# In a fused attention, feed-forward and expert kernel, two-source SBUF work is moved from GpSimd to VectorE for the feed-forward part

## The chip, the core and the metric

The kernel runs on one core of a Trainium2 chip. The metric is the device time of one execution in microseconds (us). Before the change the median of three runs is 783.74 us (783.47 to 784.02).

## What is computed

The reference runs three stages one after the other: a linear attention with exponential features, a layer that mixes along the sequence and then applies a feed-forward network, and an expert layer. Cut to what matters here:

```python
def phi(x):
    proj = np.einsum('bhsd,df->bhsf', x, w_phi)          # b 4, h 8, s 576, d 64, f 128
    proj = proj - np.max(np.abs(proj), axis=-1, keepdims=True)
    return np.concatenate([np.exp(proj), np.exp(-proj)], axis=-1)
# attention: x = (phi(q) @ (phi(k)^T v)) / (phi(q) . sum phi(k) + 1e-6)      -> (4, 576, 512)

h = x.transpose(0, 2, 1) @ U @ V                          # rank 32
u = x + h.transpose(0, 2, 1)
x = u + np.maximum(u @ w_ch1, 0.0) @ w_ch2                # 512 -> 2048 -> 512

# experts: each token takes one of 8 (argmax of x @ w_gate, or the one of the token before)
out[b, s] = p[e] * (np.maximum(x[b, s] @ w1[e], 0.0) @ w2[e])
```

The weights `U`, `V`, `w_ch1` and `w_ch2` come as float64; the kernel narrows them to float32 itself. `w1` and `w2` are float32.

## The kernel before

**Stages.** The program is one long list of instructions, built by a Python planner. The attention stage runs to about 203 us. The feed-forward network follows as twelve items: the 2048 hidden features are cut into four units (`ffn_units`, each of 512 features), and each unit is applied to three pieces of 768 tokens (`NP = 3`); a piece has two token blocks of 384 (`TW`). Item 0 is spread through the attention stage. Eight expert items follow (two units for each batch entry, blocks of 288). In the trace, items 1 to 2 take 206 to 272.6 us, items 3 to 5 take 272.6 to 372.4, items 6 to 8 take 372.4 to 466.4, and items 9 to 11 run on to 562 us, with the routing of the tokens to experts between their steps.

**One matrix product.** TensorE multiplies float32 in three passes: each operand is split in a high part (float32r) and the rest, and `three` (lines 965 to 976) issues high by high, high by rest and rest by high. So each weight piece `f` needs a copy on ScalarE (`w_end`, line 344) and a subtraction (lines 345 and 346, which ends in line 71 or line 338); each token block needs the same (`x_end`, lines 512 and 515). Items 4 to 11 use seven products in place of eight for the first matrix (`seven_steps`), which needs sums and differences of weight blocks (`sums`, lines 374 to 376) and of token blocks (`x_sums`, `sub`, lines 548 to 551).

**Work on the result.** The sums of `seven_steps` (line 943, `u`, `psf`), the ReLU with its split (line 959 on ScalarE, line 945 on VectorE) and the addition to `y` (line 943, `y`) read PSUM. TensorE needs them soon.

**Narrowing a weight piece.** `fetch` (lines 311 to 331) takes a raw float64 piece of 128x512 that SyncE's queue has loaded, and `narrow` (lines 80 to 104) turns it to float32 in six VectorE instructions, lines 89, 92, 95, 97, 99 and 102, and one addition on GpSimd in two halves of 256 (`in_halves`, line 71). Line 89 clears the sign bit of the high words. Units 1, 2 and 3 are narrowed beside the items: eight pieces each.

**Who does what.** `either` (lines 196 to 217) gives a two-source operation on SBUF to GpSimd or to VectorE, whichever the planner's clock has done sooner, with one microsecond (`BIAS`) against VectorE. On GpSimd it is cut in halves; on VectorE it is one instruction, line 338 for 512 columns. GpSimd's queue also issues the loads of saved token blocks from DRAM (`x_load`, line 578); SyncE's queue issues the stores of blocks (line 518), the raw weights (line 305) and `row` loads (line 544).

**What sets the order.** The planner keeps a modelled clock for each engine (`free`), a time for each buffer (`touched`) and one for the work that `either` places (`port`). Every engine runs its instructions in the order in which they were emitted. `gate` (lines 182 to 194) emits a step when its modelled end is not later than TensorE's modelled time plus `SLACK`, which has a value for each engine and each step of an item; for VectorE it is 0 to 2.5 us. When TensorE needs a weight or a block that isn't there, `until` (line 250) forces it out. `fetch` waits until two of the eight `row` buffers are free (line 315), and `x_load` and `x_end` take from nine token-block buffers (`xfree`). The expert items don't use `fetch`.

Of the kernel before, what the change touches and what calls it, by code (L numbers as in the profile page):

```python
# [39 lines left out]
def model(ctx, tc, kq, vx, wphi, ident, up, vp, wff, wg, wmoe1, wmoe2, rconst, outT):  # L40
# [23 lines left out]
    rawfree = [raw_p.tile([128, 1024], U32, name=f"raw{n}") for n in range(2)]  # L64

    pauses = [False]
    landed, wire = [0.0], [0.0]

    def paused(eng, **kw):
# [5 lines left out]
    def in_halves(eng, dst, a, b, n, op):  # L75

        for sl in (slice(0, n // 2), slice(n // 2, n)):
            paused(eng, out=dst[:, sl], in0=a[:, sl], in1=b[:, sl], op=op)

    def narrow(dst, raw, p, n, a=None, own=None):  # L80


        hw, lw = raw[:, 1::2], raw[:, 0::2]
        fine = own is not None
        own = own or [rows.pop(0) for _ in range(1 + (a is None))]
        a = own[1][:p, :n] if a is None else a
        b = own[0][:p, :n]
        au, bu = a.bitcast(U32), b.bitcast(U32)
        nc.vector.tensor_scalar(out=au, in0=hw, scalar1=0x7FFFFFFF, scalar2=None, op0=ALU.bitwise_and)  # L89
        if fine:  # L90
            yield
        nc.vector.tensor_scalar(out=b, in0=a, scalar1=F64_LO, scalar2=F64_MAX, op0=ALU.max, op1=ALU.min)
        if fine:
            yield
        nc.vector.tensor_scalar(out=au, in0=bu, scalar1=3, scalar2=0x3FFFFFFF, op0=ALU.logical_shift_left, op1=ALU.bitwise_and)
        yield
        nc.vector.scalar_tensor_tensor(out=au, in0=hw, scalar=0xC0000000, in1=au, op0=ALU.bitwise_and, op1=ALU.bitwise_or)
        yield
        nc.vector.tensor_scalar(out=bu, in0=au, scalar1=0xFF800000, scalar2=None, op0=ALU.bitwise_and)
        if fine:  # L100
            yield
        nc.vector.scalar_tensor_tensor(out=b, in0=lw, scalar=2.0 ** -52, in1=b, op0=ALU.mult, op1=ALU.mult)  # L102
        in_halves(nc.gpsimd, dst, a, b, n, ALU.add)
        rows.extend(own)

    def load_small(src, p, n):
# [36 lines left out]
    def x_tile(pool, n):  # L143
# [19 lines left out]
             "ACT": (0.3, 1.8, 1.8, 1.8, 0.5, 0.0, 0.5, 2.0, 2.0, 2.0, 2.0, 2.0, 2.0, 2.0, 2.0),  # L163
             "POOL": (2.0,) * 15}
    BIAS = 1.0
    at_step = [7]

    def cost(eng, n):
        return {"DVE": (0.075 + n / 960) * 1.15, "ACT": 0.17 + n / 1330, "POOL": 0.05 + n / 340}[eng]

    def of(eng):
        return "POOL" if eng is nc.gpsimd else "DVE"
# [9 lines left out]
    def gate(eng, dur, *keys):  # L182

        if not late:
            yield "step"
        while late and not force[0]:
            at = max([free[eng]] + [touched.get(id(k), 0.0) for k in keys])
            if at + (0.0 if eng == "POOL" else dur) <= free["PE"] + SLACK[eng][at_step[0]]:
                break
            yield "wait"  # L190
        emitted[0] += 1
        force[0] = False
        if late:
            book(eng, dur, *keys)

    def either(eng, n, *keys):

        if not late:
            yield "step"
            emitted[0] += 1  # L200
            return eng
        while True:
            best = None
            for e, name, bias in ((nc.gpsimd, "POOL", 0.0), (nc.vector, "DVE", BIAS)):
                dur = cost(name, n)
                at = max([free[name], port[0]] + [touched.get(id(k), 0.0) for k in keys])
                ok = at + (0.0 if name == "POOL" else dur) <= free["PE"] + SLACK[name][at_step[0]]
                if (ok or force[0]) and (best is None or at + dur + bias < best[0]):
                    best = (at + dur + bias, e, name, dur)
            if best is not None:  # L210
                break
            yield "wait"
        emitted[0] += 1
        force[0] = False
        free[best[2]] = max(free[best[2]], port[0])
        port[0] = book(best[2], best[3], *keys)
        return best[1]
# [89 lines left out]
            raws.append((u, name, t))  # L307

    pieces = {}

    def fetch(u, names):

        for name in names:
            raw_dma()
            while not raws or raws[0][:2] != (u, name) or len(rows) < 2:
                yield "blocked"
                raw_dma()
            t, f = raws.pop(0)[2], rows.pop(0)
            if wff.dtype == F32:
                yield from gate("POOL", cost("POOL", 512), t, f)  # L320
                nc.gpsimd.tensor_copy(out=f[:, :512], in_=t.bitcast(F32)[:, :512])
            else:
                g = yield from take(rows)
                parts = narrow(f[:, :512], t, 128, 512, f[:, :512], [g])
                for n_ in range(6):
                    yield from gate("DVE", 0.72 if n_ in (3, 5) else 0.46, t, f)
                    next(parts, None)
                book("POOL", cost("POOL", 512), f)
            rawfree.append(t)
            raw_dma()  # L330
            pieces[u, name] = f

# [173 lines left out]
    def x_end(key, s, r, keep, own=None, then=None):  # L506

        x = xo.setdefault(key, {})[s] = yield from take(xfree)
        n_ = CH if key[0] == "m" else TW
        keys = (x,) if own is None else (x, own)  # L510
        yield from gate("ACT", cost("ACT", 2 * n_), *keys)
        nc.scalar.copy(out=x[:, 0, :, :n_], in_=r)  # L512
        for k in range(2):
            use = yield from either(nc.gpsimd, n_, *keys)
            paused(use, out=x[:, 1, k, :n_], in0=r[:, k], in1=f32(x[:, 0, k, :n_]), op=ALU.subtract)
        if keep:
            def send():
                nc.sync.dma_start(out=f32(xd[key[1]][XD.index(s)]), in_=f32(x))
                if late:
                    transfer(768)  # L520
            later(x, send)
        xdone.add((key, s))
        if then is not None:
            then()
# [10 lines left out]
    def x_sums(key, due):  # L535
# [2 lines left out]

        def load(s):
            r = got[s] = yield from take(rows)  # L540
            while touched.get(id(r), 0.0) > free["PE"] + 0.5 and not force[0]:
                yield "wait"
            k, t = spot(key, s)
            nc.sync.dma_start(out=as_x(r), in_=ud[:, k, t])
            emitted[0] += 1
            touched[id(r)] = max(transfer(384), touched.get(id(r), 0.0) + 3.5)
# [21 lines left out]
        rows.append(got["B22"])  # L568
        end("T4", got["B21"])

    def x_load(key, names=XS):

        for s in names:
            x = xo.setdefault(key, {})[s] = yield from take(xfree)
            while touched.get(id(x), 0.0) > free["PE"] + 0.3 and not force[0]:
                yield "wait"
            yield from gate("POOL", 0.6, x)
# [333 lines left out]

    def x_first(key, due):

        yield from x_load(key, ("B11",))
        yield from x_sums(key, due)
        yield from x_load(key, ("B21", "B22"))

    def x_next(i):

# [315 lines left out]
    def side(i, step, steps):  # L1235

        u, b = items[i]
        if not late:
            return
        pauses[0] = i < NP or i > nf - NP  # L1240
        at_step[0] = 8 if steps == 16 else step
        k = units.index(u)
        if u.kind == "moe":
# [257 lines left out]
```

## Time and profile before

| | |
|---|---|
| median of three runs | 783.74 us |
| profiled execution | 781.76 us |
| its span, first to last instruction | 779.7 us |
| mean granted TensorE clock | 0.999 |
| TensorE busy | 763.8 us, 98% of the span |
| VectorE busy | 482.7 us, 62% |
| GpSimd busy | 362.2 us, 46% |
| ScalarE busy | 300.7 us, 39% |

The profiled execution is 1.98 us under the median, and its span is 2.06 us shorter than its own time. A difference worked out in the trace is taken off the median as it is. In rows of groups the first number after the bar is the busy time of all instructions of the group, the second the mean of one. A line can be a helper's: line 71 is every GpSimd subtraction or addition on SBUF, line 943 every VectorE sum that reads PSUM.

### The profile page before, as it was taken

The numbers are of one execution on the slowest core, as the hardware profiler recorded it, in microseconds if no ns is written. First come the engines' busy times: TensorE is split into PE (matmuls) and PEld (weight loads), VectorE is DVE, ScalarE is ACT, GpSimd is POOL, SyncE is SP. The second block draws the span as 40 slices with busy tenths as digits, with TensorE's granted clock in tenths as the row PEclk, the third lists the DMA queues.
The fourth block names the chain that finished last, engine by engine and source line by source line (L and its number), as shares of the span: only waits on it lengthen the run. The fifth ranks groups of instructions, "written<-read, shape, count | busy, mean of one in ns | idle before, by whom it ended". The sixth has DMA issues, their size and how long they took to land.

```text
span 779.7 us, 19252 instructions
## 1 busy us (share of the span) xinstructions
PE 763.8 (98%) x7776; PEld 741.6 (95%) x7776; DVE 482.7 (62%) x921; ACT 300.7 (39%) x682; POOL 362.2 (46%) x463
## 2 busy tenths in 40 slices
PE   8999999999999999899999999999999999999997
PEld 6899988999999999898999999999999999999997
DVE  7899999742488779897796865255643632203212
ACT  6667777652322131212213122023365164333420
POOL 1212423112477567574278532003566777866612
PEclk9999999999999999999999999999999999999999
DMA  6434556222342727591634807442453433434201
GB/s 200 153 125 160 207 178 227 71 104 82 136 169 82 277 88 278 195 340 65 228 120 162 301 1 270 152 146 82 131 186 97 133 102 102 125 122 127 79 1 63
DMA packets 45115, 114.34 MB, mean 147 GB/s; under 512 B 5024, under 2 KB 21536, under 8 KB 45024
## 3 DMA queue, kind: packets, MB, share of 16 engines
q1 hardware_dynamic: 36416, 82.74, 30.9%
q0 software_dynamic: 5152, 26.89, 10.2%
q10 hardware_dynamic: 3456, 3.46, 1.3%
q8 instruction: 62, 1.02, 0.5%
q14 instruction: 29, 0.24, 0.1%
HBM read 81.47 MB, written 31.60 MB: 145 GB/s over the span
## 4 chain that ended last, share of the span: by engine, by line
PE 82%; DVE 9%; issue 4%; POOL 2%; ACT 2%; POOLq 0%; DMA 0%; DVEq 0%; ACTq 0%
PE psf L1087 11%; PE psf L1089 11%; PE psf L1088 11%; PE psf L972 11%; PE psf L971 11%; PE psf L973 10%; PE kv L709 4%; PE pj L676 3%; PE num L743 3%; PE tq L723 2%; POOL row L71 1%; PE tps L769 1%; PE utps L786 1%; DVE row L89 1%; DVE pg L680 1%
## 5 line engine op out<-in xcount | busy, mean ns | idle before, releaser
L1087 PE MATMUL psf<-hhi,w 128*128 128x384 f32 (+1 forms) x640 | 204.6, 320 | 1.6 <-DVE hlo L945 1.6
L1088 PE MATMUL psf<-hhi,w 128*128 128x384 f32 (+1 forms) x640 | 203.7, 318 | 0.0
L1089 PE MATMUL psf<-hlo,w 128*128 128x384 f32 (+1 forms) x640 | 203.6, 318 | 0.0
L971 PE MATMUL psf<-x,w 128*128 128x384 f32 (+1 forms) x608 | 194.2, 319 | 3.0 <-DVE u L943 3.0
L972 PE MATMUL psf<-x,w 128*128 128x384 f32 (+1 forms) x608 | 193.9, 319 | 0.0
L973 PE MATMUL psf<-x,w 128*128 128x384 f32 (+1 forms) x608 | 193.9, 319 | 0.0
L945 DVE SCALAR_TENSOR_TENSOR hlo<-psf,hhi 128x384 fp32r<-128x384 f32 (+1 forms) x160 | 78.9, 514 | 145.9 <-ACT hhi L959 145.6
L71 POOL TENSOR_TENSOR w<-row,w 128x256 fp32r<-128x256 f32 x122 | 97.3, 809 | 92.8 <-ACT w L344 39.1
L959 ACT ACTIVATE hhi<-psf 128x384 fp32r<-128x384 f32 (+1 forms) x160 | 70.3, 461 | 176.6 <-PE psf L973 85.3
L71 POOL TENSOR_TENSOR row<-row,row 128x256 f32<-128x256 f32 (+1 forms) x105 | 89.1, 869 | 99.4 <-DVE row L102 91.1
L1087 PEld LDWEIGHTS psf<-hhi,w 128*128 128x128 f32 x640 | 120.1, 188 | 3.4 <-DVE hlo L945 2.3
L943 DVE TENSOR_TENSOR y<-psf,y 128x384 f32<-128x384 f32 (+1 forms) x128 | 67.0, 528 | 86.0 <-PE psf L1089 82.0
L1088 PEld LDWEIGHTS psf<-hhi,w 128*128 128x128 f32 x640 | 120.1, 188 | 0.0
L1089 PEld LDWEIGHTS psf<-hlo,w 128*128 128x128 f32 x640 | 120.1, 188 | 0.0
L971 PEld LDWEIGHTS psf<-x,w 128*128 128x128 f32 x608 | 114.3, 188 | 4.9 <-DVE u L943 4.0
L972 PEld LDWEIGHTS psf<-x,w 128*128 128x128 f32 x608 | 114.2, 188 | 0.3 <-POOL x L71 0.3
L973 PEld LDWEIGHTS psf<-x,w 128*128 128x128 f32 x608 | 114.2, 188 | 0.0
L71 POOL TENSOR_TENSOR x<-y,x 128x288 fp32r<-128x288 f32 (+1 forms) x56 | 51.9, 930 | 85.2 <-ACT x L512 78.2
L71 POOL TENSOR_TENSOR w<-raw,w 128x256 fp32r<-128x256 f32 x72 | 54.5, 757 | 32.6 <-ACT w L344 16.1
L344 ACT CAST w<-row 128x512 fp32r<-128x512 f32 x61 | 36.3, 622 | 76.7 <-POOL row L71 31.5
L679 DVE TENSOR_REDUCE mx<-pj 128x6 f32<-128x768 f32 (+2 forms) x49 | 45.8, 935 | 5.8 <-PE pj L676 5.7
L680 DVE TENSOR_TENSOR pg<-pj,mx 128x768 f32<-128x768 f32 (+2 forms) x49 | 46.1, 941 | 2.5
(110 smaller groups left out, 950.3 us busy)
## 6 DMA issues: line engine op xcount, KB each, us to landing
x<-xd POOLq DMA_DIRECT2D x34, 768.0 KB, 6.4
xd<-x SPq DMA_DIRECT2D x22, 768.0 KB, 4.5
raw<-in_wff SPq DMA_DIRECT2D x32, 512.0 KB, 3.3
raw<-in_wmoe SPq DMA_DIRECT2D x37, 256.0 KB, 2.7
kq<-in_kq SPq DMA_DIRECT2D x14, 576.0 KB, 3.9
row<-in_wmoe SPq DMA_DIRECT2D x27, 256.0 KB, 2.9
vt<-in_vx SPq DMA_DIRECT2D x16, 325.0 KB, 3.3
ud<-y SPq DMA_DIRECT2D x4, 1152.0 KB, 6.8
```

The costliest lines, as they stand in the source:

```text
L71: eng.tensor_tensor(**kw)
L679: nc.vector.tensor_reduce(out=mx[:, :, sl], in_=ps[:, :, sl], axis=AX, op=ALU.max, apply_absolute_value=True)
L680: nc.vector.tensor_tensor(out=p[:, :, sl], in0=ps[:, :, sl], in1=mx[:, :, sl].unsqueeze(3).to_broadcast([128, 2, m, 128]), op=ALU.subtract)
L943: nc.vector.tensor_tensor(**kw)
L945: nc.vector.scalar_tensor_tensor(op1=op1, **kw)
L959: at = act(lambda: nc.scalar.activation(out=hhi, in_=src, func=ACTF.Relu), n_, ready)
L971: nc.tensor.matmul(ps, lhsT=w[:, 0, c], rhs=x[:, 0, k, :n_], start=(first and k == 0), stop=False, skip_group_check=True)
L972: nc.tensor.matmul(ps, lhsT=w[:, 0, c], rhs=x[:, 1, k, :n_], start=False, stop=False, skip_group_check=True)
L973: nc.tensor.matmul(ps, lhsT=w[:, 1, c], rhs=x[:, 0, k, :n_], start=False, stop=(stop and k == 1), skip_group_check=True)
L1087: nc.tensor.matmul(ps, lhsT=wh, rhs=hhi, start=(k == 0), stop=False)
L1088: nc.tensor.matmul(ps, lhsT=wl, rhs=hhi, start=False, stop=False)
L1089: nc.tensor.matmul(ps, lhsT=wh, rhs=hlo, start=False, stop=(k == 3))
```

## The change

Up to the last but one feed-forward item (`lean`, item index below 11) `either` may choose VectorE alone, so that every sum, difference and split of weights and token blocks that was issued to GpSimd goes to VectorE as one instruction. GpSimd keeps the loads of line 578. The last addition of `narrow` goes through `either` as well. Line 89, which cleared the sign on VectorE, becomes an `Abs` on ScalarE for the pieces that `fetch` narrows. In the planner, VectorE's cost loses a factor of 1.15, the narrowing steps are booked at 0.37 and 0.62 in place of 0.46 and 0.72, and a VectorE step under `gate` is booked on `port` too. Two counters (`wanted`) keep rows and token-block buffers free for the start of a new set of token blocks (`x_first`). The attention stage, item 11 and the expert items keep their rules, apart from the new costs.

```diff
--- before.py
+++ after.py
@@ -64,6 +64,7 @@
     rawfree = [raw_p.tile([128, 1024], U32, name=f"raw{n}") for n in range(2)]
 
     pauses = [False]
+    pick = [nc.gpsimd]
     landed, wire = [0.0], [0.0]
 
     def paused(eng, **kw):
@@ -86,9 +87,11 @@
         a = own[1][:p, :n] if a is None else a
         b = own[0][:p, :n]
         au, bu = a.bitcast(U32), b.bitcast(U32)
-        nc.vector.tensor_scalar(out=au, in0=hw, scalar1=0x7FFFFFFF, scalar2=None, op0=ALU.bitwise_and)
         if fine:
+            nc.scalar.activation(out=a, in_=hw.bitcast(F32), func=ACTF.Abs)
             yield
+        else:
+            nc.vector.tensor_scalar(out=au, in0=hw, scalar1=0x7FFFFFFF, scalar2=None, op0=ALU.bitwise_and)
         nc.vector.tensor_scalar(out=b, in0=a, scalar1=F64_LO, scalar2=F64_MAX, op0=ALU.max, op1=ALU.min)
         if fine:
             yield
@@ -100,7 +103,12 @@
         if fine:
             yield
         nc.vector.scalar_tensor_tensor(out=b, in0=lw, scalar=2.0 ** -52, in1=b, op0=ALU.mult, op1=ALU.mult)
-        in_halves(nc.gpsimd, dst, a, b, n, ALU.add)
+        if fine:
+            yield
+        if pick[0] is nc.vector:
+            nc.vector.tensor_tensor(out=dst, in0=a, in1=b, op=ALU.add)
+        else:
+            in_halves(nc.gpsimd, dst, a, b, n, ALU.add)
         rows.extend(own)
 
     def load_small(src, p, n):
@@ -163,10 +171,11 @@
              "ACT": (0.3, 1.8, 1.8, 1.8, 0.5, 0.0, 0.5, 2.0, 2.0, 2.0, 2.0, 2.0, 2.0, 2.0, 2.0),
              "POOL": (2.0,) * 15}
     BIAS = 1.0
+    lean = [False]
     at_step = [7]
 
     def cost(eng, n):
-        return {"DVE": (0.075 + n / 960) * 1.15, "ACT": 0.17 + n / 1330, "POOL": 0.05 + n / 340}[eng]
+        return {"DVE": 0.085 + n / 960, "ACT": 0.17 + n / 1330, "POOL": 0.05 + n / 340}[eng]
 
     def of(eng):
         return "POOL" if eng is nc.gpsimd else "DVE"
@@ -184,14 +193,18 @@
         if not late:
             yield "step"
         while late and not force[0]:
-            at = max([free[eng]] + [touched.get(id(k), 0.0) for k in keys])
+            at = max([free[eng], port[0] if eng == "DVE" else 0.0] + [touched.get(id(k), 0.0) for k in keys])
             if at + (0.0 if eng == "POOL" else dur) <= free["PE"] + SLACK[eng][at_step[0]]:
                 break
             yield "wait"
         emitted[0] += 1
         force[0] = False
         if late:
-            book(eng, dur, *keys)
+            if eng == "DVE":
+                free[eng] = max(free[eng], port[0])
+            at = book(eng, dur, *keys)
+            if eng == "DVE":
+                port[0] = at
 
     def either(eng, n, *keys):
 
@@ -204,8 +217,8 @@
             for e, name, bias in ((nc.gpsimd, "POOL", 0.0), (nc.vector, "DVE", BIAS)):
                 dur = cost(name, n)
                 at = max([free[name], port[0]] + [touched.get(id(k), 0.0) for k in keys])
-                ok = at + (0.0 if name == "POOL" else dur) <= free["PE"] + SLACK[name][at_step[0]]
-                if (ok or force[0]) and (best is None or at + dur + bias < best[0]):
+                ok = (name == "DVE" or not lean[0]) and at + (0.0 if name == "POOL" else dur) <= free["PE"] + SLACK[name][at_step[0]]
+                if (ok or force[0] and (name == "DVE" or not lean[0])) and (best is None or at + dur + bias < best[0]):
                     best = (at + dur + bias, e, name, dur)
             if best is not None:
                 break
@@ -307,12 +320,13 @@
             raws.append((u, name, t))
 
     pieces = {}
+    wanted = [0, 0]
 
     def fetch(u, names):
 
         for name in names:
             raw_dma()
-            while not raws or raws[0][:2] != (u, name) or len(rows) < 2:
+            while not raws or raws[0][:2] != (u, name) or len(rows) < 2 + wanted[0]:
                 yield "blocked"
                 raw_dma()
             t, f = raws.pop(0)[2], rows.pop(0)
@@ -323,10 +337,18 @@
                 g = yield from take(rows)
                 parts = narrow(f[:, :512], t, 128, 512, f[:, :512], [g])
                 for n_ in range(6):
-                    yield from gate("DVE", 0.72 if n_ in (3, 5) else 0.46, t, f)
+                    if n_:
+                        yield from gate("DVE", 0.62 if n_ in (3, 5) else 0.37, t, f)
+                    else:
+                        yield from gate("ACT", cost("ACT", 512), t, f)
                     next(parts, None)
-                book("POOL", cost("POOL", 512), f)
-            rawfree.append(t)
+                rawfree.append(t)
+                raw_dma()
+                pick[0] = yield from either(nc.gpsimd, 512, f)
+                next(parts, None)
+                pick[0] = nc.gpsimd
+            if wff.dtype == F32:
+                rawfree.append(t)
             raw_dma()
             pieces[u, name] = f
 
@@ -506,6 +528,7 @@
     def x_end(key, s, r, keep, own=None, then=None):
 
         x = xo.setdefault(key, {})[s] = yield from take(xfree)
+        wanted[1] -= then is not None
         n_ = CH if key[0] == "m" else TW
         keys = (x,) if own is None else (x, own)
         yield from gate("ACT", cost("ACT", 2 * n_), *keys)
@@ -538,6 +561,7 @@
 
         def load(s):
             r = got[s] = yield from take(rows)
+            wanted[0] -= 1
             while touched.get(id(r), 0.0) > free["PE"] + 0.5 and not force[0]:
                 yield "wait"
             k, t = spot(key, s)
@@ -568,10 +592,13 @@
         rows.append(got["B22"])
         end("T4", got["B21"])
 
-    def x_load(key, names=XS):
+    def x_load(key, names=XS, first=False):
 
         for s in names:
+            while not first and len(xfree) <= wanted[1]:
+                yield "blocked"
             x = xo.setdefault(key, {})[s] = yield from take(xfree)
+            wanted[1] -= first
             while touched.get(id(x), 0.0) > free["PE"] + 0.3 and not force[0]:
                 yield "wait"
             yield from gate("POOL", 0.6, x)
@@ -911,9 +938,11 @@
 
     def x_first(key, due):
 
-        yield from x_load(key, ("B11",))
+        wanted[0] += 4
+        wanted[1] += 7
+        yield from x_load(key, ("B11",), True)
         yield from x_sums(key, due)
-        yield from x_load(key, ("B21", "B22"))
+        yield from x_load(key, ("B21", "B22"), True)
 
     def x_next(i):
 
@@ -1238,6 +1267,7 @@
         if not late:
             return
         pauses[0] = i < NP or i > nf - NP
+        lean[0] = i < nf - 1
         at_step[0] = 8 if steps == 16 else step
         k = units.index(u)
         if u.kind == "moe":
```

## Rows read from the trace of the kernel before

**Rows 1.** The page's engine table: busy us, share, instructions.

```profile
PE 763.8 (98%) x7776; PEld 741.6 (95%) x7776; DVE 482.7 (62%) x921; ACT 300.7 (39%) x682; POOL 362.2 (46%) x463
```

**Rows 2.** TensorE's waits, 195 to 525 us: us, times, longest.

```profile
PE psf L971 <- DVE u L943: 3.0, 3, 2.0
PE psf L1087 <- DVE hlo L945: 1.6, 1, 1.6
```

**Rows 3.** TensorE's timeline, first and last of four waits: start, us, instruction.

```profile
314.35 0.44 PE L971 MATMUL psf<-x,w 128*128 128x384 f32 x1 [2.00 <-DVE u L943]
...
411.83 0.45 PE L971 MATMUL psf<-x,w 128*128 128x384 f32 x1 [0.67 <-DVE u L943]
```

**Rows 4.** Engines' busy us (instructions) in items 1-8, then 3-5.

```profile
206.00:466.40 260.40, 255.71 (x1468) 254.02 (x1467) 207.94 (x342) 65.76 (x125) 162.43 (x192) 1.00 0.51 183
272.60:372.40 99.80, 95.78 (x549) 94.71 (x548) 82.72 (x129) 25.36 (x48) 61.72 (x71) 1.00 0.53 189
```

**Rows 5.** Timeline of VectorE, then GpSimd, around 335 us.

```profile
334.50 4.49 DVE L89 TENSOR_SCALAR row<-raw 128x512 uint32<-128x512 uint32 x1
...
334.75 3.94 POOL L71 TENSOR_TENSOR x<-row,x 128x384 fp32r<-128x384 f32 x4
```

**Rows 6.** VectorE's timeline where GpSimd is idle.

```profile
432.27 0.69 DVE L97 SCALAR_TENSOR_TENSOR row<-raw,row 128x512 uint32<-128x512 uint32 x1
432.97 0.56 DVE L943 TENSOR_TENSOR y<-psf,y 128x384 f32<-128x384 f32 x1
433.44 0.42 DVE L99 TENSOR_SCALAR row<-row 128x512 uint32<-128x512 uint32 x1
433.89 0.69 DVE L102 SCALAR_TENSOR_TENSOR row<-raw,row 128x512 f32<-128x512 uint32 x1
```

**Rows 7.** VectorE's narrowing by form, 195 to 525 us: busy us, mean ns.

```profile
L97 DVE SCALAR_TENSOR_TENSOR row<-raw,row 128x512 uint32<-128x512 uint32 x24 | 21.6, 900 | 0.4
L102 DVE SCALAR_TENSOR_TENSOR row<-raw,row 128x512 f32<-128x512 uint32 x24 | 19.8, 826 | 0.3
L95 DVE TENSOR_SCALAR row<-row 128x512 uint32<-128x512 uint32 x24 | 18.8, 784 | 0.6
L89 DVE TENSOR_SCALAR row<-raw 128x512 uint32<-128x512 uint32 x24 | 16.9, 703 | 0.0
L92 DVE TENSOR_SCALAR row<-row 128x512 f32<-128x512 f32 x24 | 16.3, 677 | 3.9 <-POOL row L71 2.8 <-DVE row L89 0.2
L99 DVE TENSOR_SCALAR row<-row 128x512 uint32<-128x512 uint32 x24 | 13.6, 567 | 0.3
```

**Rows 8.** GpSimd's work by form, 195 to 525 us.

```profile
L71 POOL TENSOR_TENSOR row<-row,row 128x256 f32<-128x256 f32 x68 | 55.8, 837 | 47.5 <-DVE row L102 44.0 <-POOL row L71 0.6 <-DVE w L338 0.6
L71 POOL TENSOR_TENSOR w<-row,w 128x256 fp32r<-128x256 f32 x56 | 47.2, 862 | 36.6 <-ACT w L344 34.4 <-POOL w L71 1.3 <-issue 0.6
L71 POOL TENSOR_TENSOR row<-row,row 128x384 f32<-128x384 f32 x21 | 22.0, 1077 | 4.8 <-DMA row<-ud 4.8
L71 POOL TENSOR_TENSOR x<-row,x 128x384 fp32r<-128x384 f32 x16 | 16.6, 1057 | 2.4 <-ACT x L512 2.4
L71 POOL TENSOR_TENSOR x<-y,x 128x384 fp32r<-128x384 f32 x12 | 12.4, 1041 | 17.4 <-ACT x L512 15.9 <-issue 1.1 <-POOL x L71 0.2
```

**Rows 9.** VectorE's splits of weights, then of tokens: ns min/median/max.

```profile
L338 DVE TENSOR_TENSOR w<-row,w x8: 681/1166/2626, 264.3 to 712.9; 128x512 fp32r<-128x512 f32 x8
...
L71 DVE TENSOR_TENSOR x<-row,x x8: 544/873/1359, 297.8 to 430.0; 128x384 fp32r<-128x384 f32 x8
```

**Rows 10.** Timeline: unit 2's last split, its second matrix's first matmul.

```profile
373.71 1.64 POOL L71 TENSOR_TENSOR w<-row,w 128x256 fp32r<-128x256 f32 x2 [6.40 <-ACT w L344]
...
388.00 0.45 PE L1087 MATMUL psf<-hhi,w 128*128 128x384 f32 x1
```

**Rows 11.** ScalarE's groups by form, whole run: copy, table load.

```profile
L344 ACT CAST w<-row 128x512 fp32r<-128x512 f32 x61 | 36.3, 622 | 76.7 <-POOL row L71 31.5 <-PE psf L1089 25.9 <-issue 14.7
...
L687 ACT ACT_TABLE_LOAD x1 | 1.3, 1283 | 1.2 <-PEq L1490 1.2
```

## Prediction

> **What bounds the kernel now.** I read the engine table first. TensorE is busy for 763.8 of 779.7 us [rows 1], so an edit that touches no matmul can gain only where TensorE stands still. The second view is TensorE's waits. From the end of the attention stage to item 9 it names four, all on VectorE: three in which a matmul waits for `u` (3.0 us together, the longest 2.0) and one for a ReLU rest, `hlo` (1.6 us) [rows 2]. The timeline places the first at 314 us and the last at 411 us; the other two lie between, in item 5 [rows 3]. The table by stages gives the same from the other side: in items 1 to 8 TensorE works 255.71 of 260.40 us, 4.69 us less than all [rows 4]. The change acts on these items and on the nearly idle items 9 and 10, so **4.7 us is the most that it can bring**, unless it reaches something that no row shows.
>
> Why is VectorE late? Its timeline beside that of GpSimd shows it. At 334.50 us line 89, one operation on 512 columns, takes 4.49 us. From 334.75 to 338.69 us GpSimd does four token splits in a row, and line 89 ends when they have ended [rows 5]. Where GpSimd is idle, an operation of the same kind takes 0.42 us and a two-source one 0.69 us [rows 6]. So VectorE and GpSimd hold each other up when both work on SBUF, and the one that came late waits for the other's whole queue. Operations that read PSUM don't show it. The planner doesn't know of this for the narrowing steps: it books 0.46 and 0.72 us for what took 0.57 to 0.90 us on average [rows 7]. Behind such an operation stand the sums that TensorE needs.
>
> The Trainium skill (SBUF — State Buffer, section Who interferes with whom) describes the same as an exclusive lock between GpSimd and a VectorE operation with two SBUF inputs or in a two-port mode; the 4.49 us beside 3.94 us agree.
>
> **The change, part by part.** All durations are from the profiled execution (781.76 us, 1.98 us under the median); I take the differences off the median of 783.74 us.
>
> *Added to VectorE.* GpSimd's forms in 195 to 525 us [rows 8]: 68 and 56 halves of 256 columns are 62 operations on 512. 21, 16 and 12 operations on 384 columns are 49 (at most: the first of the 12 may have been emitted before the change sets in). Undisturbed on VectorE they take 0.68 and 0.54 us, the least in [rows 9]. The next instruction may start 0.09 us before the end (432.97 + 0.56 against 433.44 [rows 6]), if it doesn't need the result. So 62 x 0.59 + 49 x 0.45 = 58.7 us, and without any overlap 62 x 0.68 + 49 x 0.54 = 68.7 us.
>
> *Taken from VectorE.* Line 89: 16.9 us [rows 7]. The time for which the other narrowing lines stood blocked, against 24 x 0.42 = 10.1 us for the one-source and 24 x 0.69 = 16.6 us for the two-source lines [rows 6, 7]: 8.7 (line 95), 6.2 (line 92), 3.5 (line 99), 5.0 (line 97) and 3.2 us (line 102), together 26.6. The splits that VectorE does already: 8 x (1.166 - 0.681) = 3.9 us for weights and 8 x (0.873 - 0.544) = 2.6 us for tokens [rows 9]. Sum: 50.0 us.
>
> *Net.* VectorE gets 58.7 - 50.0 = 8.7 us more, 18.7 at the upper end. In items 1 to 8 it was busy for 207.94 us [rows 4]; now it is 216.6 to 226.6 us of the 255.7 that are left without waits, **85 to 89%**. The fullest stage is items 3 to 5 with 82.72 us [rows 4]; a third of the net is 2.9 to 6.2, which makes 85.6 to 88.9 of 95.8 us, 89 to 93%. This is full, but it fits. What isn't ready in time has cover: the last split of unit 2 ended at 375.35 us, and its second matrix begins at 388.00 us, 12.65 us later [rows 10]; that is more than a unit's share of the net.
>
> *The four waits.* The planner's bookings now come near what VectorE will take when nobody blocks it: 0.618 us (0.085 + 512/960) against 0.59, and 0.485 (0.085 + 384/960) against 0.45 for the moved work. For narrowing they are short: start to start line 97 took 0.70 and line 99 0.45 us [rows 6], against 0.62 and 0.37 booked, 0.08 us on each of five steps, 0.40 per piece. The waits stood where two to five blocked operations lay before `u`. Without the blocks the rest is at most a piece's 0.40 us at each of the four places, 1.6 us, and nothing at best; I take 1.0 us, as some of it falls into VectorE's own gaps. The gain is 4.7 - 1.0 = **3.7 us**.
>
> *Sign on ScalarE.* The trace has no `Abs`; the nearest row is ScalarE's copy of 512 columns, 0.622 us [rows 11]. 24 of them are 14.9 us on an engine that is busy for 65.76 of 260.40 us [rows 4]. The cover is ScalarE's idle time. An `Abs` that stands ahead of a ReLU delays it by up to 0.62 us, in the worst case 24 times; a gain can come where a narrowing chain starts sooner, since VectorE is no longer needed for it. I take zero: the planner's gate for ScalarE weighs it as it does the copies, and no wait of TensorE names ScalarE [rows 2].
>
> ScalarE loaded a function table once in the whole run, 1.283 us [rows 11]. The Trainium skill (ScalarE: Activation LUTs, section Table sets: the hidden batching unit) says that cheap functions, `abs` among them, are in every set, so by it no second load comes; if `Abs` needed one each way, ScalarE would have 48 x 1.283 = 61.6 us more. No run here shows which yet.
>
> *Queues.* GpSimd's queue keeps the token loads alone, so that none stands behind a split any more. SyncE's stores of token blocks now wait for VectorE's split in place of GpSimd's; its raw weight loads follow line 102 as before. No wait of TensorE names a transfer [rows 2], so I count nothing either way; a stage short of token blocks would show as a wait for `x`. The counters `wanted` are waits of the planner, not of an engine: weights start later while a new token set takes its four rows, inside the cover of 12.65 us.
>
> **Rivals.**
>
> *The waits move (no change).* VectorE stays at 89% or more in items 3 to 5, and each narrowing piece runs 0.40 us behind the plan. The waits then come back at other steps at about their size, 4 us of the 4.7: 783.1 us. For it: the slack of the planner is unchanged, and was already too little. Against it: each wait that I followed had a blocked operation before it.
>
> *The plan runs away (slower).* VectorE's queue isn't allowed to drain: at 0.40 us a piece, 24 pieces are 9.6 us behind the plan. If VectorE's gaps take none of this, it lands on `u` and `hlo`: 783.7 - 4.7 + 9.6 = 788.6 us. The place is the start of items 4, 5, 7 and 8, and it decides from the point where VectorE has less idle time than a stage's lag, 8 x 0.40 = 3.2 us; items 3 to 5 have 95.8 - 88.9 = 6.9 us left at the upper load.
>
> *VectorE is full (slower).* If the blocked time doesn't come back (because it is VectorE's own cost at those places), its load in items 3 to 5 is 82.7 less a third of 16.9 and plus a third of 68.7 us, 100.0 of 95.8 us; the 4.2 us and the like in items 6 to 8 come on top of the old time less its waits: 783.7 - 4.7 + 2 x 4.2 = 787.4 us. Against it stand [rows 5, 6].
>
> The Trainium skill (Perfetto Trace Analysis, section Optimizing Scalar/DVE Operations) says that work of a saturated VectorE may be given to ScalarE or even GpSimd, and warns that between VectorE and GpSimd this might not help; by its first half this change goes the wrong way, by its second the right one. The rows so far speak for the second.
>
> *It doesn't act as said.* Table loads, or token blocks held back by `wanted`: some us slower, or no change because most operations stay where they are; about 785 us.
>
> **How the numbers follow.** Forecast 0.57 (780.0 us, its own range 779.0 to 782.1), the waits move 0.21, the plan runs away 0.10, VectorE is full 0.07, not as said 0.05. The likeliest gives 783.7 - 3.7 = **780.0 us**. The lower end is all of the 4.7 us and the spread of the runs of 0.3, 778.7 us. Upwards I leave out the upper part of the two full-VectorE cases: 786.5 us. A measurement of this kernel can tell about 0.2% (1.6 us) from no change. Faster: the forecast, 0.57. Same: the moved waits and half of the last case, 0.23. Slower: 0.20.
>
> **What would show it.** Right: no GpSimd line 71 between 210 and 525 us; narrowing lines at 0.42 to 0.45 and 0.69 us on average; VectorE busy for about 217 us in items 1 to 8; 24 `Abs` near 0.62 us and one table load; TensorE's waits there 1.0 us in place of 4.7, and the attention stage and the expert items at their old lengths. Wrong: narrowing lines that stay long without GpSimd; waits for `u` or `hlo` of 0.5 us or more at each start of an item; matmuls that wait for `w` or `x`, or a VectorE over 92% in items 3 to 5.

## The result and the profile after

The change makes the kernel faster: 776.28 us (775.96 to 778.38) against 783.57 us (782.78 to 784.02), medians of six runs each. The ratio is 0.9916 with a 95% interval of 0.9902 to 0.9929: 0.84% less, clear of the interval. The profiled execution took 776.39 us with a span of 774.6 us. Lines have moved: 943 is now 972 (sums on PSUM), 945 is 974 (`hlo`), 71 is 72, 338 is 360, 971 is 1000 and 1087 is 1116; 89 is 91 (the sign, on ScalarE), 92 to 102 are 95 to 105, and 109 is the new addition.

The engine table of the page, against [rows 1]; then the table by stages, items 1 to 8 and items 3 to 5, against [rows 4] (stretch, length, TensorE, weight load, VectorE, ScalarE and GpSimd busy us):

```profile
PE 762.7 (98%) x7776; PEld 742.1 (96%) x7776; DVE 492.0 (64%) x1005; ACT 315.3 (41%) x706; POOL 210.5 (27%) x293
```

```profile
206.00:466.40 260.40, 260.40 (x1505) 260.37 (x1504) 218.49 (x428) 81.91 (x152) 14.19 (x26) 1.00 0.51 183
272.60:372.40 99.80, 99.80 (x578) 99.80 (x577) 85.03 (x168) 32.78 (x61) 3.72 (x7) 1.00 0.47 173
```

TensorE works without a break where it stood still for 4.69 us; its view of waits names none in the feed-forward part, where [rows 2] had two lines. In items 1 to 8 VectorE has 10.5 us more, GpSimd 148 us less; the same stretch of time now holds 37 more of TensorE's matmuls.

VectorE's groups by form in 195 to 525 us, against [rows 7] and [rows 9] (busy us, mean ns), and under them GpSimd's, against [rows 8]:

```profile
L360 DVE TENSOR_TENSOR w<-row,w 128x512 fp32r<-128x512 f32 x34 | 22.2, 683 | 3.3 <-ACT w L366 3.3
L109 DVE TENSOR_TENSOR row<-row,row 128x512 f32<-128x512 f32 x24 | 16.5, 688 | 0.5
L100 DVE SCALAR_TENSOR_TENSOR row<-raw,row 128x512 uint32<-128x512 uint32 x24 | 16.5, 688 | 0.5
L105 DVE SCALAR_TENSOR_TENSOR row<-raw,row 128x512 f32<-128x512 uint32 x24 | 16.5, 687 | 0.5
...
L102 DVE TENSOR_SCALAR row<-row 128x512 uint32<-128x512 uint32 x24 | 10.2, 423 | 0.5
L98 DVE TENSOR_SCALAR row<-row 128x512 uint32<-128x512 uint32 x24 | 10.2, 423 | 0.5
L95 DVE TENSOR_SCALAR row<-row 128x512 f32<-128x512 f32 x24 | 10.1, 420 | 6.6 <-ACT row L91 6.4
```

```profile
L605 POOL DMA_DIRECT2D x<-xd x34 | 18.2, 536 | 277.9 <-PE psf L1002 204.6 <-DVE row L95 49.4 <-DVE hlo L974 7.8
L72 POOL TENSOR_TENSOR x<-y,x 128x384 fp32r<-128x384 f32 x3 | 3.0, 1018 | 15.9 <-ACT x L535 15.9
```

The narrowing lines stand at 0.42 and 0.69 us on average, where they had 0.57 to 0.90. All 62 operations on 512 columns have moved, and 46 on 384; three splits of token blocks stayed on GpSimd.

How much came from the feed-forward part can be read without any busy time. TensorE's matmuls are the same and in the same order in both kernels, so the distance from the start of the last `utps` matmuls of the attention stage to the first transposes of the routing is a clean measure. TensorE's timeline of after:

```profile
206.51 0.54 PE L813 MATMUL utps<-vs,ts 128*128 128x320 f32 x2
...
518.32 0.71 PE L1168 MATMUL psf<-id_sb,row 128*128 128x128 f32 x5
```

and of before:

```profile
205.67 0.54 PE L786 MATMUL utps<-vs,ts 128*128 128x320 f32 x2
...
523.58 0.71 PE L1139 MATMUL psf<-id_sb,row 128*128 128x128 f32 x5
```

That is 311.81 against 317.91 us: **6.10 us** in one execution each, though TensorE's idle time was shown as 4.69 us. I call the distance D. The three kernels of the table below that have no wait there take 311.81 and 311.82 us, which I call the floor.

### The profile page after: what moved, and what is told of

It is laid out like the page before. It is cut to its first block, busy times and chain, and to the rows that moved or that the text cites. A ratio compares the mean times of both kernels' runs of the same rounds, so it can differ in the third digit from the quotient of the medians.

```text
span 774.6 us, 19121 instructions
## 1 busy us (share of the span) xinstructions
PE 762.7 (98%) x7776; PEld 742.1 (96%) x7776; DVE 492.0 (64%) x1005; ACT 315.3 (41%) x706; POOL 210.5 (27%) x293
## 4 chain that ended last, share of the span: by engine, by line
PE 93%; DVE 4%; ACT 2%; DMA 1%; issue 0%; SPq 0%; ACTq 0%; DVEq 0%
PE psf L1116 13%; PE psf L1118 13%; PE psf L1117 13%; PE psf L1001 12%; PE psf L1002 12%; PE psf L1000 12%; PE kv L736 4%; PE num L770 3%; PE pj L703 3%; PE tq L750 2%; PE tps L796 1%; PE utps L813 1%; DVE pg L707 1%; PE utps L808 1%; DVE mx L706 1%; DMA vt<-in_vx 1%
## 5 line engine op out<-in xcount | busy, mean ns | idle before, releaser
L1117 PE MATMUL psf<-hhi,w 128*128 128x384 f32 (+1 forms) x640 | 203.7, 318 | 0.0
L1117 PEld LDWEIGHTS psf<-hhi,w 128*128 128x128 f32 x640 | 120.1, 188 | 0.0
L605 POOL DMA_DIRECT2D x<-xd x34 | 18.2, 536 | 277.9 <-PE psf L1002 204.6
L72 POOL TENSOR_TENSOR w<-row,w 128x256 fp32r<-128x256 f32 x66 | 50.2, 765 | 56.4 <-ACT w L390 38.2
L72 POOL TENSOR_TENSOR x<-y,x 128x288 fp32r<-128x288 f32 (+1 forms) x47 | 42.1, 901 | 84.4 <-ACT x L535 78.5
L736 PE MATMUL kv<-vt,ek 128*64 128x65 f32 (+1 forms) x1152 | 47.1, 230 | 0.6 <-DMA vt<-in_vx 0.6
```

Source lines behind the costliest of these rows:

```text
L72: eng.tensor_tensor(**kw)
L736: nc.tensor.matmul(out[c], lhsT=e[:, half, i, c], rhs=rhs, start=(tl == 0 and half == 0), stop=(tl == 8 and half == 1), skip_group_check=True)
L1117: nc.tensor.matmul(ps, lhsT=wl, rhs=hhi, start=False, stop=False)
```

## The experiments

All times but the first are medians; each ratio is to runs of the kernel before that were timed beside it. D is that of the one profiled execution, "over the floor" is D less 311.81 us, and "idle shown" is the sum of TensorE's waits in its trace. Medians of kernels that ran beside different runs of before are best compared by their ratios.

| kernel | us | ratio, 95% interval | D, us | over the floor | idle shown |
|---|---|---|---|---|---|
| before, first execution profiled | 781.76 | | 317.91 | 6.10 | 4.69 |
| before again | 782.84 | 0.9996 [0.9986, 1.0006] | 318.57 | 6.76 | 4.15 |
| after | 776.28 | 0.9916 [0.9902, 0.9929] | 311.81 | 0 | 0 |
| extra reading work on GpSimd | 808.31 | 1.0321 [1.0307, 1.0336] | 342.96 | 31.1 | 22.8 |
| extra writing work on GpSimd | 789.24 | 1.0077 [1.0060, 1.0093] | 324.39 | 12.6 | 7.2 |
| all old prices | 785.20 | 1.0021 [1.0011, 1.0031] | 320.35 | 8.5 | 5.2 |
| old prices, GpSimd back | 781.52 | 0.9972 [0.9960, 0.9983] | 316.87 | 5.1 | 2.8 |
| sign on VectorE | 776.19 | 0.9911 [0.9896, 0.9925] | 311.82 | 0 | 0 |
| old narrowing prices | 782.47 | 0.9983 [0.9973, 0.9993] | 317.27 | 5.5 | 3.4 |
| old factor | 781.66 | 0.9978 [0.9964, 0.9992] | 315.98 | 4.2 | 3.5 |
| long waits put in | 786.97 | 1.0065 [1.0041, 1.0088] | 321.86 | 10.0 | 6.6 |
| short waits put in | 780.06 | 0.9963 [0.9949, 0.9976] | 315.45 | 3.6 | 3.1 |
| tokens on GpSimd | 776.82 | 0.9925 [0.9912, 0.9938] | 311.82 | 0 | 0 |
| weights on GpSimd | 785.37 | 1.0029 [1.0017, 1.0040] | 320.03 | 8.2 | 5.9 |

**1. The kernel before, once more.** No edit.

> The kernel before, unchanged, to see how its waits differ from one execution to another. The profiled execution of before took 781.76 us, 1.8 us under its median of 783.57. Theory A1 (GpSimd and VectorE meet on SBUF by chance, so the waits of TensorE in items 1 to 8 differ from run to run): time near 783.6 us, and this execution's waits start to start differ from the 6.1 us of the first one, by about as much as its time differs from 781.76. Rival A2 (the missing 1.8 us lie in the attention stage or the tail): items 1 to 8 again show 6.1 us within 0.3, and the difference of time lies elsewhere.

Ten runs lie between 781.67 and 783.77 us. The profiled one (783.19 us) has nearly the first wait of the first execution in its timeline, but not the same matmuls after it:

```profile
312.69 0.34 PE L973 MATMUL psf<-x,w 128*128 128x384 f32 x1
315.04 0.52 PE L971 MATMUL psf<-x,w 128*128 128x384 f32 x1 [2.01 <-DVE u L943]
315.35 0.52 PE L972 MATMUL psf<-x,w 128*128 128x384 f32 x1
315.67 0.52 PE L973 MATMUL psf<-x,w 128*128 128x384 f32 x1
```

Matmuls start 0.32 us apart behind the wait of 2.01 us, where 0.17 is usual. Its table by stages gives the granted clock (third number from the end):

```profile
315.00:318.70 3.70, 3.66 (x12) 3.66 (x13) 3.53 (x8) 0.00 (x0) 1.50 (x3) 0.54 1.06 375
318.70:321.00 2.30, 2.30 (x15) 2.30 (x14) 1.88 (x4) 0.29 (x1) 1.31 (x3) 1.00 0.54 202
```

Behind this wait it stood for most of 3.7 us at the lower of its two levels, 1.2 GHz. Behind the wait of 2.00 us of the first execution [rows 3] it stayed at 2.4 GHz:

```profile
314.00:318.00 4.00, 3.65 (x21) 3.65 (x22) 3.83 (x9) 0.00 (x0) 1.82 (x3) 1.00 1.06 360
```

Neither theory is quite right: TensorE's waits are even 0.54 us shorter than in the first execution (4.15 against 4.69), and what follows one of them makes D 0.66 us longer, 318.57 us. The attention stage ended 0.68 us later (206.35 against 205.67).

**2. Work on GpSimd that nobody uses.** On the changed kernel, after each ReLU (`k` = 1) and each addition to `y` (`k` = 2) of items 1 to 10:

```diff
+            nc.gpsimd.tensor_copy(out=junk[1], in_=src)
+            for _ in range(k):
+                nc.gpsimd.tensor_tensor(out=junk[0][:, 0:256], in0=junk[0][:, 256:512], in1=junk[0][:, 512:768], op=ALU.mult)
```

> The changed kernel with extra work on GpSimd in items 1 to 10 that nobody uses: one product of 256 columns after each ReLU and two after each addition to y, on tiles of its own, so GpSimd reads SBUF for about as long as before (some 19 us of each 31 us item) while VectorE's work and the plan are those of the changed kernel. Theory A (GpSimd's SBUF work blocks VectorE): VectorE's narrowing lines go from 0.42 and 0.69 us to 0.55 us or more and 0.8 us or more on average, and waits of TensorE for u or hlo come back, 3 us or more: 779 us or more. Rival B (the planner's new prices and order brought the gain): 776.3 us within 1 us, as the order is unchanged.

808.31 us. With the plan untouched, TensorE waits again, and VectorE's lines are as slow as before the change (TensorE's waits, then VectorE's groups by form):

```profile
PE psf L1009 <- DVE u L973: 17.4, 5, 6.4
PE psf L1009 <- DVE y L973: 4.7, 2, 3.8
```

```profile
L101 DVE SCALAR_TENSOR_TENSOR row<-raw,row 128x512 uint32<-128x512 uint32 x24 | 21.5, 898 | 0.5
L106 DVE SCALAR_TENSOR_TENSOR row<-raw,row 128x512 f32<-128x512 uint32 x24 | 20.5, 853 | 0.5
...
L99 DVE TENSOR_SCALAR row<-row 128x512 uint32<-128x512 uint32 x24 | 16.7, 695 | 0.5
```

So extra work on GpSimd, with the plan untouched, is enough to block VectorE and to stop TensorE. The size can't be carried over: GpSimd was busy for 188 us between 206 and 466 us, more than the 162 of before, and the plan knew nothing of it.

**3. The same with a memset, which reads nothing.**

```diff
-                nc.gpsimd.tensor_tensor(out=junk[0][:, 0:256], in0=junk[0][:, 256:512], in1=junk[0][:, 512:768], op=ALU.mult)
+                nc.gpsimd.memset(junk[0], 1.0)
```

> As the one with extra work on GpSimd, at the same places, but each extra operation is a memset of 768 columns, which writes SBUF and reads nothing. If only GpSimd's reading blocks VectorE's two-source lines: lines 100 and 105 and the sums stay at 0.69 us and only the one-source lines may grow; under 1 us of waits, 776.3 to 777.5 us. If GpSimd's queue as such is what costs (token loads stand behind extra work): waits for x appear, and the time grows as with the reading work, 779 us or more.

789.24 us. Only the one-source lines grew, as the first theory has it. The time I gave for it was wrong: 7.2 us of waits come back, all for `u`:

```profile
L99 DVE TENSOR_SCALAR row<-row 128x512 uint32<-128x512 uint32 x24 | 17.8, 744 | 0.5
...
L101 DVE SCALAR_TENSOR_TENSOR row<-raw,row 128x512 uint32<-128x512 uint32 x24 | 16.5, 687 | 0.5
L106 DVE SCALAR_TENSOR_TENSOR row<-raw,row 128x512 f32<-128x512 uint32 x24 | 16.4, 685 | 0.5
```

No wait of TensorE for `x` appeared, so token loads that stand behind the extra work aren't it. That the slower lines alone bring the 7.2 us isn't shown, for the copy ahead of each memset reads `hhi` or `y`, and ScalarE and VectorE waited for it:

```profile
ACT hhi L996 <- POOL junk L987: 4.4, 2, 2.8
DVE y L973 <- POOL junk L987: 1.5, 1, 1.5
```

The Trainium skill (SBUF — State Buffer, section Who interferes with whom) says that a two-source VectorE operation contends only with a GpSimd operation that reads, and a one-source operation in a two-port mode with any; 687 and 744 ns here, 898 and 695 in the second kernel, agree.

**4. The old prices.** VectorE keeps all work.

```diff
-        return {"DVE": 0.085 + n / 960, ...
+        return {"DVE": (0.075 + n / 960) * 1.15, ...
-                        yield from gate("DVE", 0.62 if n_ in (3, 5) else 0.37, t, f)
+                        yield from gate("DVE", 0.72 if n_ in (3, 5) else 0.46, t, f)
```

and `gate` without `port`.

> The changed kernel with the planner's old prices: the factor 1.15 on VectorE, 0.46 and 0.72 us for narrowing, and no booking of gated steps on port. VectorE still has all two-source work, ScalarE the sign. Theory A: most of the gain stays, as nobody blocks VectorE; but the plan gives VectorE less work per item, so weights may come late: 776.3 to 778.5 us. Rival B (prices brought the gain): 780 us or more.

785.20 us, 0.2% slower than before. VectorE isn't blocked (its narrowing lines are at 0.42 and 0.69 us), yet TensorE waits, now for weights:

```profile
PE psf L998 <- DVE w L356: 4.2, 1, 4.2
PE psf L1113 <- DVE w L356: 1.0, 1, 1.0
```

Theory A fell as I had put it: unblocking VectorE is not enough. At the old prices the plan hands VectorE less in items 3 to 5 (81.67 us busy against 85.03), and unit 2's weights are late at item 6.

**5. Old prices, and GpSimd allowed again.** Against the fourth kernel one line differs:

```diff
-        lean[0] = i < nf - 1
+        lean[0] = False
```

> The changed kernel with the old prices, as the one at 785.2 us, but GpSimd may take two-source work again; the sign stays on ScalarE. Against that one only the engine differs. Theory A (blocking): VectorE's narrowing lines are again 0.55 to 0.9 us, TensorE waits for u or hlo and not for w: 782 to 787 us. Rival (with the old prices the plan alone sets the time): waits for w as before this step, about 5 us in sum, narrowing lines at any length.

781.52 us. The waits are for `u` again (2.8 us), none for `w`, and the narrowing lines are blocked:

```profile
L100 DVE SCALAR_TENSOR_TENSOR row<-raw,row 128x512 uint32<-128x512 uint32 x24 | 30.0, 1251 | 0.6
L105 DVE SCALAR_TENSOR_TENSOR row<-raw,row 128x512 f32<-128x512 uint32 x24 | 20.0, 834 | 0.4
```

So **at the old prices the move of the engine alone costs 3.8 us** (the ratios 1.0021 and 0.9972 are 0.49% apart). The counterpart, the new prices with GpSimd allowed throughout, doesn't exist, since the planner comes to a dead end there; the eleventh and twelfth kernels allow one half each. This kernel is 0.3% quicker than before, though GpSimd has its work back; what is left of the change in it are the sign, the choice of an engine for the last addition of `narrow`, and details of the planner, and which of them does it wasn't tried.

**6. The sign on VectorE.**

```diff
-            nc.scalar.activation(out=a, in_=hw.bitcast(F32), func=ACTF.Abs)
+            nc.vector.tensor_scalar(out=au, in0=hw, scalar1=0x7FFFFFFF, scalar2=None, op0=ALU.bitwise_and)
-                    if n_:
-                        yield from gate("DVE", 0.62 if n_ in (3, 5) else 0.37, t, f)
-                    else:
-                        yield from gate("ACT", cost("ACT", 512), t, f)
+                    yield from gate("DVE", 0.62 if n_ in (3, 5) else 0.37, t, f)
```

> The changed kernel with the sign cleared on VectorE as before, all else changed. VectorE gets 24 x 0.42 = 10 us more, 228 of 260 us in items 1 to 8. Theory D (VectorE is so full that this step was needed): weights come late, waits for w of 2 us or more: 779 us or more. Rival (it fits, the step is a trifle): no waits, 776.0 to 777.2 us.

776.19 us, no waits, D at the floor. VectorE carries the 10 us easily (225.72 of 260.40 us). At the new prices this part of the change brings nothing.

**7 and 8. Each price alone.** One of the two price lines of the fourth kernel in each; `port` stays.

> The changed kernel, with the planner's old prices for the narrowing steps alone (0.46 and 0.72 us, near the 0.45 and 0.70 that the trace shows start to start). Theory P1 (the plan needs narrowing booked short, to fit): waits for w as with all old prices, 780 us or more. Rival P2 (the factor of 1.15 was what held work back): 776.0 to 777.5 us.

> The changed kernel with the factor of 1.15 on VectorE's price back (512 columns at 0.70 in place of 0.62 us; measured 0.59 start to start), narrowing at the new prices. Theory P1: 776.0 to 777.5 us. Rival P2: waits for w, 780 us or more.

Each alone brings the waits for `w` back, 3.4 and 3.5 us, so both theories were half right: either price is enough to make the plan late. TensorE's waits in the seventh kernel:

```profile
PE psf L1117 <- DVE w L360: 2.7, 1, 2.7
PE psf L1002 <- DVE w L360: 0.6, 1, 0.6
```

The two are a pair for the clock as well. Behind a wait of 2.74 us the seventh was granted 0.57 of full speed, behind 2.73 us the eighth 1.00 (tables by stages of the one and of the other), and D differs by 1.29 us:

```profile
388.50:392.50 4.00, 3.94 (x14) 3.94 (x15) 2.87 (x7) 0.00 (x0) 0.00 (x0) 0.57 0.29 112
```

```profile
388.80:392.80 4.00, 3.96 (x22) 3.83 (x23) 3.93 (x8) 0.00 (x0) 0.00 (x0) 1.00 0.53 202
```

**9 and 10. What a wait costs, by itself.** Ten copies, or seven, on VectorE ahead of the first sums of items 9 and 10 of the changed kernel:

```diff
+        if i in (9, 10):
+            for _ in range(10):
+                nc.vector.tensor_copy(out=junk[0], in_=done["b", 0][0])
```

> The changed kernel with ten copies of 384 columns from PSUM to a tile that nobody reads, on VectorE ahead of the first sums of items 9 and 10, where VectorE is else nearly idle. TensorE then waits for u about 2.2 us in each of the two items. Theory C (a wait costs more than the idle time shown: 0.28 us from the pipelined ends and, after the longer waits, matmuls at half the granted clock, some 0.15 us each for about 11 to 20 of them): 2 x (2.2 + 0.28) = 5.0 us, and up to 2 x 1.7 us more in some executions: 781.2 to 784.7 us, stretches with a granted clock near 0.5. Rival (a wait costs what it shows): 2 x 2.2: 780.7 us.

> The same with seven copies, so that TensorE waits about 0.8 us in each of the two items. Theory C: no half clock after waits this short (none was seen behind waits of 0.4 to 1.7 us), so 2 x (0.8 + 0.28) = 2.2 us: 778.5 us. Rival (a wait costs what it shows): 1.6 us, 777.9 us.

The waits came out longer than meant, two of 3.32 and two of 1.54 us. The short ones show 3.08 us idle and cost 3.64 us in D, 0.28 more for each wait, at a clock of 1.00; the median is 3.2 us above that of the eleventh kernel, which was timed beside it and has no wait (below). The long ones show 6.64 us and cost 10.0 us in D; the clock fell behind both:

```profile
472.00:475.20 3.20, 3.06 (x10) 3.06 (x11) 1.25 (x4) 0.00 (x0) 0.00 (x0) 0.53 0.53 195
508.00:512.70 4.70, 4.46 (x17) 4.46 (x18) 2.67 (x6) 0.00 (x0) 0.53 (x1) 0.64 0.42 162
```

The median is 10.2 us above that of the eleventh. Less the idle time and 0.28 us for each wait, 2.85 us are left, 1.4 for each fall of the clock. Theory C holds for the 0.28 us and for the clock.

**11 and 12. One half of the move each.** The eleventh lets `either` give 384 columns (`n < 512`) to GpSimd again, the twelfth 512 columns (`n == 512`); prices are new.

```diff
-                ok = (name == "DVE" or not lean[0]) and ...
+                ok = (name == "DVE" or not lean[0] or n < 512) and ...
```

> The changed kernel, but either may give the work on 384 columns (token blocks) to GpSimd again; the weights' 512 columns stay on VectorE. Theory A (any GpSimd work on SBUF blocks VectorE): about 49 GpSimd operations of 1.05 us, narrowing lines between 0.42 and 0.6 us, VectorE some 22 us less loaded, waits of 1 to 4 us: 777 to 781 us. Rival (VectorE's load is the limit, and less of it helps or does nothing): 776.0 to 776.6 us.

> The counterpart of the kernel with tokens on GpSimd: either may give the work on 512 columns (weights) to GpSimd again, in halves of 256; the token blocks' 384 columns stay on VectorE, all prices new. Theory A' (blocking counts where GpSimd's operations fall in the middle of the narrowing, and the weights' do): some 60 operations, about 100 us of GpSimd's time, narrowing lines at 0.55 us or more, waits for u or w: 779 to 784 us, from the end of the attention stage to the first transposes of the routing 314 us or more. Rival (either half of the move is enough, since the new prices order the work well): 776 to 777 us, 311.8 us between these two places.

With tokens on GpSimd there is no wait, and the time is that of after: my theory of "any GpSimd work" fell. GpSimd has 69 us of work in items 1 to 8, but the narrowing shows little of it: 0.49 us at most on average for a one-source line, 0.70 for a two-source one (by form, VectorE, then GpSimd):

```profile
L98 DVE TENSOR_SCALAR row<-row 128x512 uint32<-128x512 uint32 x24 | 11.8, 494 | 0.8
```

```profile
L72 POOL TENSOR_TENSOR row<-row,row 128x384 f32<-128x384 f32 x24 | 25.8, 1110 | 94.7 <-DMA row<-ud 94.7
```

With weights on GpSimd the time is 785.37 us, line 98 at 724 ns, and weights come late:

```profile
PE psf L1116 <- ACT w L366: 5.6, 1, 5.6
PE psf L1117 <- POOL w L72: 0.3, 1, 0.3
```

At the new prices the move of the weights' work is the half that counts. Whether they come late there because VectorE is blocked in their narrowing or because GpSimd is slow at their splits isn't separated.

The two `wanted` counters have no part in it: with them left at zero, all engines get the same instructions in the same order.

## Why the prediction was wrong

The forecast was 780.0 us, with 778.7 as the lower end; it became 776.28. The direction and the mechanism were right, the size of the gain was not: 7.29 us where I had 3.7.

- *What bounds the kernel.* The four waits were the right place and all of them are gone. The step that failed is **"4.7 us is the most that it can bring"**. I read the loss off TensorE's busy time [rows 4]; the distance between the two places shows 6.10 us in the same execution. The missing 1.41 us are the refill behind each wait (0.28 us, measured alone in the tenth kernel; four waits make 1.1) and a fifth stop of 0.3 us at 388 us, ahead of the second line of [rows 10]. The matmuls' view shows it as no idle time; the weight load has it (before):

```profile
387.67 0.34 PE L973 MATMUL psf<-x,w 128*128 128x384 f32 x1
388.00 0.19 PEld L1087 LDWEIGHTS psf<-hhi,w 128*128 128x128 f32 x1 [0.31 <-DVE hlo L945]
```

The ends of matmuls are modelled and overlap the next: a matmul is drawn 0.33 us long and the next starts 0.17 us later, so each wait hides some of its own length. The Trainium skill (Perfetto Trace Analysis, section Tensor Engine Instruction (MATMUL, LD_WEIGHTS)) says that these ends are estimated and not observed; the 6.10 us beside 4.69 us of idle time agree.

- *The difference taken off the median.* I used one execution that was 1.8 us quicker than the median, and let its waits stand for all. A second one had 0.66 us more in the same stretch, with matmuls at the lower clock behind the 2.01 us wait. This term was missing altogether. It had 0.68 us more in the attention stage too, but that is no gain of the change: in after the stage ended at 206.51 us, later than in either execution of before (205.67 and 206.35).
- *The four waits' rest.* I left 1.0 us for a plan that books narrowing too short. Nothing was left. The lag of 0.40 us per piece is there (the bookings are below the durations), and I take it that VectorE's gaps absorb it; no run isolates this.
- *The sum.* Of the 3.6 us by which the forecast gain was short, 1.0 is the rest that I left, 1.41 the hidden part of the waits and 0.66 the second execution's longer D: 3.07 us. The other 0.5 us stays open: the second execution of before and the profiled one of after are 6.80 us apart (783.19 against 776.39), 6.76 of it in D, and the medians are 0.49 us further apart than these two.
- *VectorE's load.* Forecast 216.6 us in items 1 to 8, measured 218.49; items 3 to 5 were given 85.6 and had 85.03. The nearness is in part luck: three operations stayed on GpSimd, the stretch holds more matmuls than before, and of the eight weight splits of [rows 9], which reach to 712.9 us, six lie before 525 us. (62 x 0.59 + 49 x 0.45 is 58.6, and the upper sum 68.6, each 0.1 less than I wrote.) The durations of moved work (0.68, 0.54) and of unblocked narrowing (0.42, 0.69) came as told.
- *The sign.* Zero was right; an `Abs` took 0.671 us on average against the 0.622 of the row, and no second table load came:

```profile
L91 ACT ACTIVATE row<-raw 128x512 f32<-128x512 f32 x24 | 16.1, 671 | 30.9 <-DMA raw<-in_wff 27.4 <-DVE row L109 3.1 <-ACT x L535 0.5
...
L714 ACT ACT_TABLE_LOAD x1 | 1.3, 1283 | 1.2 <-PEq L1520 1.2
```

- *The prices.* I wrote that the bookings come near the durations and counted this as calm. The runs show it to be a condition of most of the gain: with either old price 3.4 us of waits for weights return and about 0.2 of the 0.84% is left, and with both, and no booking on `port`, the move is slower than the kernel before. None of my rivals is this one: VectorE isn't full there (81.67 of 99.80 us in items 3 to 5), the plan holds its work back. The cover of 12.65 us that I read off the old trace [rows 10] was no cover there, since it belongs to the old plan: the seventh and eighth kernels wait at its first matmuls (L1117).
- *The tokens.* I counted their 49 operations among what had to move. They needn't have.

Shown are the blocking of VectorE by GpSimd's reading work and the stop of TensorE that follows (second kernel), the prices (fourth, seventh and eighth) and the cost of a wait (ninth and tenth). The booking on `port` wasn't tried by itself. Why the attention stage's end differs from one execution to the next, by 0.68 us in the two of before, is open.

## What to carry to other kernels

Where a planner sets the order, a move of work and the prices that describe it are one change: without its prices the move looked like a loss. Count what a stop of TensorE costs from start to start between two fixed matmuls, never from its busy time, and look at a second execution before one trace stands for the median. Of two engines that meet on SBUF, part the work that matters: here it was enough to move that on the weights, whose narrowing was blocked; the tokens' could have stayed.

## What the runs showed of the hardware

- TensorE's granted clock fell to its lower level behind waits of 2.01, 2.74, 3.32 and 5.63 us and stayed at 2.4 GHz behind waits of 2.00 and 2.73 us in other runs; behind waits of 1.5 to 1.7 us it never fell here. A fall cost 1.3 to 1.4 us of D (1.29 between the eighth and the seventh kernel, 1.4 for each of two in the ninth).
- One VectorE instruction stood behind several GpSimd operations in a row (4.49 us beside four that took 3.94 us, [rows 5]), not only behind the one that ran.
- GpSimd memsets slowed one-source VectorE work (0.42 to 0.74 us in the third kernel) and left two-source work alone (0.69 us).
